# Two of eight Strassen pairs in plain products, in an attention and feed-forward kernel on one core

## The chip, the cores and the metric

The kernel runs on one core of one Trainium2 chip. The metric is the device time of one execution in microseconds (us); 727.54 us is the median of three runs of the kernel before (723.6 to 728.09).

## The reference

Eight batches of 8 heads, 576 tokens, head dimension 64, with 32 packed queries `p` per head. Two attentions in a row, then a feed-forward net with ELU on all 4608 tokens:

```
p_packed = softmax(p k^T / 8) v             # per batch and head: 32 x 64
x = softmax(q p_packed^T / 8) p_packed      # per batch and head: 576 x 64
h = x @ w_in                                # 4608 x 512 @ 512 x 2048
g = where(h > 0, h, exp(min(h, 0)) - 1)
out = g @ w_out                             # 4608 x 2048 @ 2048 x 512
```

The weights arrive as 64-bit floats, all else as 32-bit ones.

## The kernel before

**Products.** A product of 32-bit numbers is made of three fast ones: each operand is split into a high part that the fast format holds and the low rest, and high x high, high x low and low x high are added in PSUM. The kernel multiplies the packed values with `w_in` first (`mstep`, L788), so `h` is the product of this matrix `m` (as `m_hi`, `m_lo`) with the second attention's weights `a` (`a_hi`, `a_lo`).

**Tiling.** 2048 hidden columns are 16 f tiles of 128 (`NF`), and a batch's 576 tokens are two windows. A stretch is one window through all f tiles. For even batches the windows have 256 and 320 tokens, for odd ones 320 and 256; the 64 tokens over 256 of an even batch are kept after ELU (`half_sb`) and finished with the 320 of the next odd batch's first window. Batches 0 and 1 are interleaved (`VISITS`), while weights are still being converted; from batch 2 on a stretch is 16 steps in a row.

**Plain steps.** One f tile: `h` into a PSUM bank (L1185, 6 matmuls), ELU on ACT and DVE, the split of `g`, and per 128 tokens three matmuls of 512 columns (`out_mm`, L1309 to L1312), summed over f in one bank per 128 tokens.

**Strassen pairs.** Seven stretches, those with 256 tokens to finish from batch 2, window 1, to batch 6, window 1, take two f tiles at a time (`strassen_pair`, L957): 256 tokens x 256 hidden by 256 hidden x 512 columns is a 2 x 2 product of blocks, made with seven block products instead of eight (Winograd's form). `g`'s sums are made on DVE (`sums`, L1049), high and low parts of seven blocks on ACT and DVE (`hi`, L277, and `lo`, L1055), and 21 matmuls of 256 columns (L1096) add into four banks (`acc`). They are issued in four groups, each an operation of its own. After the eighth pair DVE puts the banks together (L1122) in `part`, and one store (L1149) writes 256 rows.

**Sums of `w_out`.** Of the seven right-hand blocks three are in `w_out` itself (`own`) and four are sums. `strassen_weights` (L889) makes the sums once a pair, 32 tiles of 256 KB in all, and stores them in DRAM (`sw_dram`, L932); each stretch loads them again (L1068) into a ring of six buffers (`sw`).

**Order.** Nothing is scheduled by hand. Each operation gets a priority (`prio`, about the step at which it is due), a cost on the engines that it may run on, what it waits for and the buffers that it takes, and `schedule()` (L165) plays the program through with these costs: a free engine takes the first operation in order of priority that is ready. `LAG` is the time after an operation's end until others may use its result, 2.2 us for a DMA. The order found is written out, and on the chip each engine runs its own list in order, waiting by semaphores. SP issues nearly all DMAs, so a DMA that waits on SP holds those behind it. Due times are numbers: `T_ATT` and `T_ATTS` for the six parts of a batch's attention (`ts`: keys, transposes, value products, the transpose of the packed values, two halves of the scores), `TM` and `TMS` for `mstep`, `T_SW` for the weights' sums, `T_SL` for how many steps ahead the sums are loaded, `LOOK_S` for how late the output products are due, `T_SE` for the last additions.

**Keys, values, queries.** From batch 1 on they are loaded in halves of 576 KB into a ring of two buffers (`kvq`): keys (L458), values (L465), queries (L477). So value loads wait for the first scores (L505, L546), query loads for the value products (L642), and the next keys for the second scores (L687).

Of the kernel before, what the change touches and what calls it, by code (L numbers as in the profile page):

```python
# [20 lines left out]
def packed_attention_elu_ffn(  # L21
# [22 lines left out]
    nc = tc.nc  # L44
# [36 lines left out]
    T_ATT, T_ATT1 = [12, 14.0, 15.0, 16.0, 17.5, 17.5], [-12, -11, -11, -10, -10, -9]  # L81
    LI, LO, LM, LOOK = 4.5, 3.0, 2.5, 3.5
    TM = [24.5, 24.5, 28.0, 28.5]
# [10 lines left out]
    T_ATTS = [[10, 8, 12.5, 11.5, 12.0, 16.5], [-4, -2, 1, 8, 18, 24.0]]  # L94
    TMS = [[22, 22, 28, 28], [25, 29, 31.5, 32.0]]
    S_FIRST, T_SW, T_SL, T_SE, LOOK_S = (2, 1), 20, 2, 4, 3.5
# [58 lines left out]
    def op(prio, on, fn, deps=(), take=(), use=(), after=(), mode=None):  # L155
        o = Op()
        o.prio, o.on, o.fn, o.deps = prio, on, fn, [d for d in deps if d is not None]
        o.after = [d for d in after if d is not None]
        o.take, o.end, o.n, o.mode = list(take), None, len(ops), mode
        for b in list(take) + list(use):  # L160
            b.users.append(o)
        ops.append(o)
        return o

    def schedule():  # L165
# [19 lines left out]
        while todo:  # L185
            for n, o in enumerate(todo[:400]):
# [14 lines left out]
                o.start, o.end = now, now + cost + LAG[e]  # L201
# [194 lines left out]
    def attention(b, ts):  # L396
# [542 lines left out]
    for u in range(NF // 2):  # L939
        strassen_weights(u)  # L940
# [16 lines left out]
    def strassen_pair(i, b, win, f):  # L957
# [92 lines left out]

        def hi(e):
            copy(e, g_b.all[:, :7 * P], blocks(1, 8))

        def lo(e):
            nc.vector.tensor_tensor(  # L1055
                out=g_b.all[:, 7 * P:], in0=blocks(1, 8), in1=g_b.all[:, :7 * P].bitcast(F32),
                op=ALU.subtract,
            )

        last = f + 2 == NF  # L1060
        x = op(i + 1, {"DVE": 0.95}, sums, done, use=[w8])
        x = run["g"] = op(i + 1, {"ACT": 0.95}, hi, [x], take=[g_b], use=[w8], after=[run["g"]])
        x = op(i + 1, {"DVE": 1.09}, lo, [x], use=[g_b, w8])
        sw = [sw_buf() for _ in range(4)]
        ld = {}
        for n in (2, 1, 0, 3):
            def load(e, n=n):
                nc.sync.dma_start(out=sw[n].t.bitcast(F32), in_=sw_dram[u, n])  # L1068

            ld[n] = run["sw"] = op(  # L1070
                i - T_SL, {"DMA": 0.7}, load, [s_ready[u, n]], take=[sw[n]], after=[run["sw"]]
            )
# [4 lines left out]
        def own(f, n):  # L1077
            return None, lambda part: wo(f, part)[:, n * H:(n + 1) * H]

        if f == 0:  # L1080
            run["acc"] = [banks(1) for _ in range(4)]
        acc = run["acc"]

        groups = (
            ((1, own(f, 0)),),
            ((6, t(2)), (3, own(f + 1, 0))),
            ((5, t(1)), (4, t(0))),
            ((2, t(3)), (7, own(f + 1, 1))),
        )
        for a, group in zip(acc, groups):  # L1090

            def mm(e, a=a, group=group):
                for n, (blk, (_, y)) in enumerate(group):
                    for k, (p, q) in enumerate(((0, 0), (0, 1), (1, 0))):
                        x0 = (7 * p + blk - 1) * P
                        nc.tensor.matmul(  # L1096
                            a.t[:, n * H:(n + 1) * H], lhsT=g_b.all[:, x0:x0 + P], rhs=y(q),
                            start=f == 0 and n == k == 0,
                            stop=last and k == 2 and n == len(group) - 1,
                        )  # L1100

            ns = [y[0] for _, y in group if y[0] is not None]
            run["out"] = op(
                i + 1 + LOOK_S, {"PE": 0.355 * len(group)}, mm, [x] + [ld[n] for n in ns],
                take=[a] if f == 0 else [],
                use=[g_b] + [sw[n] for n in ns] + ([] if f == 0 else [a]), after=[run["out"]],
            )
            a.last = run["out"]
        if last:
# [5 lines left out]
            def two(x):  # L1115
                return x.unsqueeze(1).to_broadcast([P, 2, H])

            def bank(n):
                return acc[n].t.rearrange("p (n e) -> p n e", e=H)

# [4 lines left out]
            def first(e):  # L1125
                copy(e, part.t[:, :H], acc[0].t[:, :H])

            def add1(e):
                add(slots(1, 1)[:, :2], two(part.t[:, :H]), bank(1))

            def add2(e):
                add(slots(0, 3), two(part.t[:, H:2 * H]), bank(2))

            def add3(e):
                add(part.t[:, H:2 * H], part.t[:, :H], acc[2].t[:, H:])

            def add4(e):
                add(slots(0, 3), slots(0, 3), bank(3))
# [3 lines left out]
            y = op(q, {"ACT": 0.35, "DVE": 0.4}, first, [acc[0].last], take=[part], use=acc[:1])  # L1142
            y = op(q, {"DVE": 0.69}, add1, [y, acc[1].last], use=[part, acc[1]])
            y = op(q, {"DVE": 0.69}, add2, [y, acc[2].last], use=[part, acc[2]])
            y = op(q, {"DVE": 0.42}, add3, [y], use=[part, acc[2]])
            y = op(q, {"DVE": 0.69}, add4, [y, acc[3].last], use=[part, acc[3]])

# [263 lines left out]
```

## Time and profile before

| what | us |
|---|---|
| median of three runs | 727.54 |
| the profiled execution's own time | 725.27 |
| its span, first to last instruction | 723.1 |
| PE busy in it (matmuls) | 694.2 |
| DVE busy | 572.7 |
| ACT busy | 437.6 |

The span is cut by what runs: loads and the first softmax to about 25 us, batches 0 and 1 with the weights' conversion, plain and Strassen stretches in turn after them, Strassen ones between 265 and 641 us, and the last window of batch 7 in plain steps to the end. PE is TensorE's matmuls, PEld its weight loads, DVE VectorE, ACT ScalarE, SP the engine that issues DMAs (SPq is its queue). A row of a group gives line, engine, operation, tiles written and read, shape and count, then busy us and the mean ns of one, then idle us ahead of them and what ended it.

### The profile page before, as it was taken

The numbers are of one execution on the slowest core, as the hardware profiler recorded it, in microseconds if no ns is written. First come the engines' busy times: TensorE is split into PE (matmuls) and PEld (weight loads), VectorE is DVE, ScalarE is ACT, GpSimd is POOL, SyncE is SP. The second block draws the span as 40 slices with busy tenths as digits, with TensorE's granted clock in tenths as the row PEclk, the third lists the DMA queues.
The fourth block names the chain that finished last, engine by engine and source line by source line (L and its number), as shares of the span: only waits on it lengthen the run. The fifth ranks groups of instructions, "written<-read, shape, count | busy, mean of one in ns | idle before, by whom it ended". The sixth has DMA issues, their size and how long they took to land.

```text
span 723.1 us, 14717 instructions
## 1 busy us (share of the span) xinstructions
PE 694.2 (96%) x5580; PEld 572.6 (79%) x5580; DVE 572.7 (79%) x1318; ACT 437.6 (61%) x936; POOL 19.4 (3%) x27
## 2 busy tenths in 40 slices
PE   2799999999998999999999999999999999999997
PEld 1445588887776888988888898888888898988886
DVE  6999998888999899755887788965787789874453
ACT  5777888786766576635566446645367556654332
POOL 0000002110111000000000000000000000000000
PEclk9999999999999999999999999999999999999999
DMA  9846546535759576705377998532468887620010
GB/s 349 292 155 206 182 145 146 132 65 126 211 108 306 213 241 206 240 4 156 112 233 233 323 289 274 183 130 67 135 197 263 284 285 256 211 82 1 0 44 30
DMA packets 66262, 128.62 MB, mean 178 GB/s; under 512 B 6544, under 2 KB 16016, under 8 KB 65936
## 3 DMA queue, kind: packets, MB, share of 16 engines
q1 hardware_dynamic: 63168, 122.18, 51.2%
q0 software_dynamic: 3024, 5.51, 5.3%
q8 instruction: 44, 0.72, 0.4%
q14 instruction: 26, 0.21, 0.1%
HBM read 104.33 MB, written 23.33 MB: 177 GB/s over the span
## 4 chain that ended last, share of the span: by engine, by line
PE 90%; DMA 6%; DVE 2%; ACT 1%; issue 0%; SPq 0%; ACTq 0%
PE psum L1096 19%; PE psum L1185 14%; PE psum L979 11%; PE psum L1309 10%; PE psum L1310 10%; PE psum L1312 10%; PE psum L1295 4%; PE psum L788 4%; DMA sw<-sw_dram 3%; DMA kvq<-in_qT 2%; PE psum L1178 2%; PE psum L642 2%; PE psum L616 1%; PE psum L687 1%; DMA k<-in_kT 1%; PE psum L546 1%
## 5 line engine op out<-in xcount | busy, mean ns | idle before, releaser
L1192 ACT ACTIVATE e<-psum 128x320 f32<-128x320 f32 (+1 forms) x144 | 59.9, 416 | 75.0 <-PE psum L1185 64.0
L1096 PE MATMUL psum<-sw,g 128*128 128x256 f32 x672 | 101.5, 284 | 3.6 <-DMA sw<-sw_dram 3.6
L1096 PEld LDWEIGHTS psum<-sw,g 128*128 128x128 f32 x672 | 88.4, 189 | 9.8 <-issue 6.0
L1201 DVE SCALAR_TENSOR_TENSOR e<-e,psum 128x256 f32<-128x256 f32 (+1 forms) x128 | 57.3, 447 | 30.0 <-ACT e L1198 29.4
L1185 PE MATMUL psum<-a_hi,m_hi 128*128 128x320 f32 (+1 forms) x256 | 79.7, 311 | 0.0
L1185 PE MATMUL psum<-a_lo,m_hi 128*128 128x320 f32 (+1 forms) x256 | 76.4, 298 | 0.0
L1185 PE MATMUL psum<-a_hi,m_lo 128*128 128x320 f32 (+1 forms) x256 | 76.3, 298 | 0.0
L1309 PE MATMUL psum<-wo_b,g 128*128 128x512 f32 x174 | 70.1, 403 | 0.0
L1310 PE MATMUL psum<-wo_b,g 128*128 128x512 f32 x174 | 68.7, 395 | 0.0
L979 PE MATMUL psum<-a_hi,m_hi 128*128 128x256 f32 (+1 forms) x224 | 67.1, 299 | 0.2 <-DVE half_sb L986 0.2
L1055 DVE TENSOR_TENSOR g<-w,g 128x896 fp32r<-128x896 f32 x56 | 60.3, 1083 | 8.4 <-ACT g L277 8.2
L1224 DVE TENSOR_TENSOR g<-e,g 128x256 fp32r<-128x256 f32 (+1 forms) x128 | 58.0, 453 | 10.7 <-ACT g L277 8.9
L277 ACT CAST g<-w 128x896 fp32r<-128x896 f32 x56 | 52.6, 939 | 22.7 <-DVE w L1049 15.9
L1198 ACT ACTIVATE e<-e 128x320 f32<-128x320 f32 (+1 forms) x144 | 64.7, 449 | 2.6
L979 PE MATMUL psum<-a_lo,m_hi 128*128 128x256 f32 (+1 forms) x224 | 65.8, 294 | 0.0
L979 PE MATMUL psum<-a_hi,m_lo 128*128 128x256 f32 (+1 forms) x224 | 65.7, 293 | 0.0
L1049 DVE TENSOR_TENSOR w<-w 128x128 f32<-128x128 f32 x168 | 56.0, 333 | 4.5
L1185 PEld LDWEIGHTS psum<-a_hi,m_hi 128*128 128x128 f32 x256 | 48.5, 189 | 10.8 <-issue 1.1
L1310 PE MATMUL psum<-wo_a,g 128*128 128x512 f32 x140 | 55.5, 396 | 0.0
L1309 PE MATMUL psum<-wo_a,g 128*128 128x512 f32 x140 | 55.4, 396 | 0.0
L1185 PEld LDWEIGHTS psum<-a_lo,m_hi 128*128 128x128 f32 x256 | 48.6, 190 | 4.5 <-issue 1.0
L1312 PE MATMUL psum<-wo_b,g 128*128 128x512 f32 x174 | 52.1, 395 | 0.0
(130 smaller groups left out, 1486.0 us busy)
## 6 DMA issues: line engine op xcount, KB each, us to landing
sw<-sw_dram SPq DMA_DIRECT2D x224, 256.0 KB, 3.7
raw<-in_w_in SPq DMA_DIRECT2D x16, 512.0 KB, 4.1
kvq<-in_v SPq DMA_DIRECT2D x16, 512.0 KB, 5.3
raw<-in_w_out SPq DMA_DIRECT2D x16, 512.0 KB, 3.5
sw_dram<-sw SPq DMA_DIRECT2D x32, 256.0 KB, 4.1
kvq<-in_kT SPq DMA_DIRECT2D x14, 576.0 KB, 4.9
kvq<-in_qT SPq DMA_DIRECT2D x14, 576.0 KB, 5.4
out<-part SPq DMA_DIRECT2D x21, 256.0 KB, 2.3
```

Source lines behind the costliest of these rows:

```text
L979: nc.tensor.matmul(ps, lhsT=m_b[p].t[:, g, o:o + P], rhs=st.a.t[q][:, g, cols], start=(n == 0), stop=(n == 3 * G - 1),)
L1049: nc.vector.tensor_tensor(out=out, in0=x, in1=y, op=o)
L1055: nc.vector.tensor_tensor(out=g_b.all[:, 7 * P:], in0=blocks(1, 8), in1=g_b.all[:, :7 * P].bitcast(F32), op=ALU.subtract,)
L1096: nc.tensor.matmul(a.t[:, n * H:(n + 1) * H], lhsT=g_b.all[:, x0:x0 + P], rhs=y(q), start=f == 0 and n == k == 0, stop=last and k == 2 and ...
L1185: nc.tensor.matmul(ps_b.t[:, :n_tok], lhsT=m_b[x].t[:, g, o:o + P], rhs=st.a.t[y][:, g, cols], start=(n == 0), stop=(n == 3 * G - 1),)
L1192: nc.scalar.activation(out=e_b.t[:, :n_tok], in_=ps_b.t[:, :n_tok], func=AF.Relu, scale=-1.0)
L1198: nc.scalar.activation(out=x, in_=x, func=AF.Exp, scale=-1.0)
L1201: nc.vector.scalar_tensor_tensor(out=out, in0=e_b.t[:, cs], scalar=-1.0, in1=ps_b.t[:, cs], op0=ALU.add, op1=ALU.max)
L1224: nc.vector.tensor_tensor(out=g_b.t[1][:, cs], in0=x, in1=g_b.t[0][:, cs].bitcast(F32), op=ALU.subtract)
L1309: nc.tensor.matmul(a.t, lhsT=g_b.t[0][:, t], rhs=wo(f, 0), start=first, stop=False)
L1310: nc.tensor.matmul(a.t, lhsT=g_b.t[0][:, t], rhs=wo(f, 1), start=False, stop=False)
L1312: nc.tensor.matmul(a.t, lhsT=g_b.t[1][:, t], rhs=wo(f, 0), start=False, stop=final)
```

## The change

In each Strassen stretch pairs 0 and 7 (`S_PLAIN`) go without the scheme. Their four blocks of `g` are split as they are (512 columns instead of 896), and twelve matmuls of 512 columns, in two groups, add the first 128 tokens' products into bank 3 and the others' into bank 2. The sums of `w_out` for these two pairs are neither made, stored nor loaded. In the other pairs the seven products are shared out among the four banks in another way, so that banks 2 and 3 hold whole halves of the result; the last additions are six instead of five. A bank is taken by the first pair that uses it.

Loads of sums are called eight steps ahead (`T_SL` 2 to 8), output products are due six steps late instead of 3.5 (`LOOK_S`), and the planner counts a load of sums with 0.8 us on the DMA and 1.5 us more until it can be used (`lag`); the same 1.5 us and a higher cost stand for keys, values and queries from batch 3 on. The due times of attention, of `mstep`, of the weights' sums and of the last additions have new numbers.

```diff
-    T_ATT, T_ATT1 = [12, 14.0, 15.0, 16.0, 17.5, 17.5], [-12, -11, -11, -10, -10, -9]
+    T_ATT, T_ATT1 = [12, 14.0, 14.5, 15.5, 17.0, 17.0], [-12, -11, -11, -10, -10, -9]
...
-    T_ATTS = [[10, 8, 12.5, 11.5, 12.0, 16.5], [-4, -2, 1, 8, 18, 24.0]]
-    S_FIRST, T_SW, T_SL, T_SE, LOOK_S = (2, 1), 20, 2, 4, 3.5
+    S_PLAIN = [0, 7]
+    T_ATTS = [[9, 7, 11.5, 8.5, 13.0, 21.5], [-4, -2, -2, 3, 14.5, 20.5]]
+    S_FIRST, T_SW, T_SL, T_SE, LOOK_S = (2, 1), 17, 8, 3, 6.0
...
-                o.start, o.end = now, now + cost + LAG[e]
+                o.start, o.end = now, now + cost + LAG[e] + o.lag
...
-                    t, {"DMA": 3.3 / len(bufs)}, lambda e, fn=fn, n=n: fn(e, n),
+                    t, {"DMA": (3.3 if b < 3 else 3.8) / len(bufs)}, lambda e, fn=fn, n=n: fn(e, n),
                     take=[x] + ([p_b] if (name, n) == ("k", 0) else []), after=[prev_ld],
+                    lag=1.5 * (b > 2),
...
     for u in range(NF // 2):
-        strassen_weights(u)
+        if u not in S_PLAIN:
+            strassen_weights(u)
...
+        plain = u in S_PLAIN
+        b0, b1 = (0, 4) if plain else (1, 8)
         def hi(e):
-            copy(e, g_b.all[:, :7 * P], blocks(1, 8))
+            copy(e, g_b.all[:, :(b1 - b0) * P], blocks(b0, b1))
...
-        x = op(i + 1, {"DVE": 0.95}, sums, done, use=[w8])
+        if not plain:
+            done = [op(i + 1, {"DVE": 0.95}, sums, done, use=[w8])]
...
+        if not plain:
+            sw = [sw_buf() for _ in range(4)]
+            for n in (2, 1, 0, 3):
...
+                ld[n] = run["sw"] = op(
+                    i - T_SL, {"DMA": 0.8}, load, [s_ready[u, n]], take=[sw[n]], after=[run["sw"]],
+                    lag=1.5,
+                )
...
         groups = (
-            ((1, own(f, 0)),),
-            ((6, t(2)), (3, own(f + 1, 0))),
-            ((5, t(1)), (4, t(0))),
-            ((2, t(3)), (7, own(f + 1, 1))),
+            ((1, own(f, 0), 0), (6, t(2), 1)),
+            ((5, t(1), 0), (4, t(0), 1)),
+            ((3, own(f + 1, 0), 0), (7, own(f + 1, 1), 1)),
+            ((2, t(3), 0),),
         )
+        if plain:
+            groups = (
+                (), (), ((1, own(f, 0, 2), 0), (3, own(f + 1, 0, 2), 0)),
+                ((0, own(f, 0, 2), 0), (2, own(f + 1, 0, 2), 0)),
+            )
...
+            cost = 1.386 if plain else 0.355 * len(group)
...
             def add4(e):
-                add(slots(0, 3), slots(0, 3), bank(3))
+                add(part.t[:, 2 * H:], part.t[:, 2 * H:], acc[2].t)
+
+            def add5(e):
+                n = 2 * H if S_PLAIN else H
+                add(part.t[:, :n], part.t[:, :n], acc[3].t[:, :n])
```

More of the change, by code (lines that the diff above doesn't have):

```diff
@@ L1061, in strassen_pair @@
-        x = op(i + 1, {"DVE": 0.95}, sums, done, use=[w8])
-        x = run["g"] = op(i + 1, {"ACT": 0.95}, hi, [x], take=[g_b], use=[w8], after=[run["g"]])
-        x = op(i + 1, {"DVE": 1.09}, lo, [x], use=[g_b, w8])
-        sw = [sw_buf() for _ in range(4)]
-        ld = {}
[L1066 to L1072, printed above, removed]
+                out=g_b.all[:, 7 * P:(7 + b1 - b0) * P], in0=blocks(b0, b1),
@@ L1113, in slots @@
                 return part.t.rearrange("p (n e) -> p n e", e=H)[:, n::step]
[L1115 to L1119, printed above, removed]
             def add(out, x, y):
```

68 lines of the change are left out of this document (42 added, 26 removed).

## The prediction

> **What bounds the kernel now.** I read the page first, then the stretches in time, then PE's waits, then the timeline at the two places where PE stood still.
>
> ```profile
> span 723.1 us, 14717 instructions
> PE 694.2 (96%) x5580; PEld 572.6 (79%) x5580; DVE 572.7 (79%) x1318; ACT 437.6 (61%) x936; POOL 19.4 (3%) x27
> core 0: us, PE busy (x) PEld busy (x) DVE busy (x) ACT busy (x) POOL busy (x), PEclk, DMA share, GB/s
> 0.00:25.00 25.00, 10.00 (x187) 5.93 (x187) 18.70 (x44) 15.99 (x31) 0.69 (x6) 1.00 0.93 346
> 25.00:227.00 202.00, 198.84 (x1509) 143.16 (x1510) 183.29 (x430) 152.72 (x360) 18.12 (x21) 0.99 0.59 161
> 227.00:235.00 8.00, 5.14 (x44) 4.08 (x42) 7.66 (x20) 4.81 (x16) 0.63 (x1) 0.97 1.06 336
> 235.00:265.00 30.00, 30.00 (x199) 24.89 (x183) 25.66 (x64) 19.07 (x49) 0.00 (x0) 0.95 0.61 216
> 265.00:641.00 376.00, 371.98 (x3256) 327.07 (x3249) 296.65 (x657) 215.14 (x407) 0.00 (x0) 1.00 0.63 203
> 641.00:723.10 82.10, 78.22 (x414) 67.43 (x412) 40.71 (x109) 29.91 (x76) 0.00 (x0) 1.00 0.06 23
> PE psum L1096 <- DMA sw<-sw_dram: 3.6, 6, 0.9
> PE psum L687 <- DMA kvq<-in_qT: 3.0, 2, 2.9
> ```
>
> PE is busy in 694.2 of 723.1 us. Of the 28.9 us without work, 15.0 lie in the first 25 us (loads and the first softmax), 3.9 after 641 us and 3.2 from 25 to 227 us; PE's order is the same in both kernels up to about 215 us. Left for this change are two places: 227 to 235 us, where 2.9 us are lost, and the Strassen stretches, 265 to 641 us, where 376.00 - 371.98 = 4.0 us are lost. The last two rows (total, times, longest) say to what: 2.9 us once to a load of queries, 3.6 us in six waits for Strassen sums read back from DRAM. DVE and ACT are not named, so work taken from them is worth nothing by itself.
>
> At the first place the wait costs more than its own length (timeline: start, time; then windows, with the granted clock third from the end):
>
> ```profile
> 231.34 0.27 PE L668 MATMUL psum<-ident,pp 128*128 128x128 f32 x1
> 234.47 1.18 PE L687 MATMUL psum<-kvq,ppT 64*32 64x288 f32 x16 [2.86 <-DMA kvq<-in_qT]
> 235.95 0.41 PE L1185 MATMUL psum<-a_lo,m_hi 128*128 128x256 f32 x1
> ...
> 240.35 0.28 PE L1185 MATMUL psum<-a_lo,m_hi 128*128 128x256 f32 x1
> 235.00:237.00 2.00, 2.00 (x22) 1.43 (x7) 0.66 (x2) 0.00 (x0) 0.00 (x0) 0.50 1.07 393
> 237.00:239.00 2.00, 2.00 (x9) 1.63 (x8) 0.58 (x3) 1.71 (x6) 0.00 (x0) 0.75 0.90 293
> ```
>
> After 2.86 us without work the granted clock is 0.50 from 235 to 237 us and 0.75 from 237 to 239, and the same matmul that takes 0.28 us at 240 takes 0.41. That is 2 x 0.50 + 2 x 0.25 = 1.5 us more.
>
> **The plain pairs.** The change turns 2 of 8 pairs in each of 7 stretches, 14 pairs, from 21 matmuls of 256 columns into 12 of 512. Their spacing, from starts in quiet places:
>
> ```profile
> 299.72 0.52 PE L1096 MATMUL psum<-wo_b,g 128*128 128x256 f32 x3
> ...
> 301.84 0.52 PE L1096 MATMUL psum<-wo_b,g 128*128 128x256 f32 x3
> 302.19 0.31 PE L1185 MATMUL psum<-a_hi,m_hi 128*128 128x320 f32 x1
> ...
> 647.48 0.39 PE L1309 MATMUL psum<-wo_a,g 128*128 128x512 f32 x1
> ...
> 648.86 0.84 PE L1312 MATMUL psum<-wo_a,g 128*128 128x512 f32 x3
> 649.54 0.30 PE L1185 MATMUL psum<-a_hi,m_hi 128*128 128x320 f32 x1
> L1310 PEld LDWEIGHTS psum<-wo_b,g 128*128 128x128 f32 x174 | 32.8, 189 | 5.0
> ```
>
> A Strassen pair's 21 matmuls (3, 15 left out, 3) take 302.19 - 299.72 = 2.47 us, 0.118 each. Nine of 512 columns (one each at 647.48, 647.71, and so on, then three) take 649.54 - 647.48 = 2.06 us, 0.229 each. A plain pair then takes 12 x 0.229 = 2.75 us, 0.28 more, and all of it is on PE, which is the path: 14 x 0.28 = **+3.9 us**. Rounding of starts makes this 3.5 to 4.3. The weight load of 189 ns lies under both; with plain pairs it lies wholly under its 229 ns.
>
> The Trainium skill (TensorE: Matmul & The Clock Gate, Back-to-back issue gap) gives another spacing for a stream of loads and matmuls, about 131 ns at 512 columns and 81 at 128. By it a plain pair would take 12 x 0.131 = 1.6 us and the change would gain on PE. This trace shows 229 ns, and the sum goes by the trace.
>
> **What leaves DVE, ACT and the queue.** Per plain pair the three sums go, and the split shrinks from 896 to 512 columns:
>
> ```profile
> L1049 DVE TENSOR_TENSOR w<-w 128x128 f32<-128x128 f32 x168 | 56.0, 333 | 4.5
> L1055 DVE TENSOR_TENSOR g<-w,g 128x896 fp32r<-128x896 f32 x56 | 60.3, 1083 | 8.4 <-ACT g L277 8.2
> L277 ACT CAST g<-w 128x896 fp32r<-128x896 f32 x56 | 52.6, 939 | 22.7 <-DVE w L1049 15.9
> L1122 DVE TENSOR_TENSOR part<-part,psum 128x512 f32<-128x512 f32 x21 | 14.4, 685 | 3.5 <-PE psum L1096 2.8 <-ACT e L1192 0.5
> sw<-sw_dram SPq DMA_DIRECT2D x224, 256.0 KB, 3.7
> ```
>
> DVE saves 56.0 / 56 = 1.0 us of sums and 1.08 - 0.69 = 0.4 us of split a pair, 14 x 1.4 = 20 us; the result of a stretch costs it one more addition of 256 columns, less than 0.69 us, 7 times. ACT saves about 14 x 0.94 x 384/896 = 5.6 us. Neither is waited for, so I cost all of it at nothing; if DVE were late somewhere it would only help. Of the read-backs 56 of 224 go, and 8 of 32 stores, for two pairs need no sums in DRAM.
>
> **The query load.** Keys, values and queries take turns in two buffers (kvq), so queries can load only after the products with the values (L642). SP's queue at this place, before, from the value loads of batch 3 to its query load and behind:
>
> ```order
> L465 DMA kvq<-in_v 128x2x512
> L469 DMA kvq<-in_v 64x256
> L932 DMA sw_dram<-sw 128x512 x8
> L477 DMA kvq<-in_qT 128x4x288 x2
> L932 DMA sw_dram<-sw 128x512 x4
> L454 DMA p<-in_pT 128x128
> ```
>
> and now (the same lines, 3 or 4 further down; L1083 is the load of sums, formerly L1068):
>
> ```order
> L468 DMA kvq<-in_v 128x2x512
> L472 DMA kvq<-in_v 64x256
> L936 DMA sw_dram<-sw 128x512 x5
> L480 DMA kvq<-in_qT 128x4x288 x2
> L936 DMA sw_dram<-sw 128x512 x8
> L1083 DMA sw<-sw_dram 128x512 x2
> ```
>
> The query load has moved ahead of three of the stores. PE's order has moved more. What stands at the first scores of batch 3 (L687), before:
>
> ```order
> L1185 MATMUL psum<-a_lo,m_hi 128x256
> L1185 MATMUL psum<-a_hi,m_lo 128x256
> L668 MATMUL psum<-ident,pp 128x128
> L687 MATMUL psum<-kvq,ppT 32x288 x8
> L1185 MATMUL psum<-a_hi,m_hi 128x256
> ```
>
> and now (L691 is the former L687, L1215 the former L1185, L1339 the former L1309):
>
> ```order
> L1215 MATMUL psum<-a_lo,m_hi 128x256
> L1215 MATMUL psum<-a_hi,m_lo 128x256
> L691 MATMUL psum<-kvq,ppT 32x288 x8
> L1339 MATMUL psum<-wo_b,g 128x512
> L1340 MATMUL psum<-wo_b,g 128x512
> ```
>
> The scores no longer follow the transpose (L668) at once. Between value products and scores stood 18 matmuls of 256 and 18 of 512 columns, 18 x 0.118 + 18 x 0.229 = 6.2 us; now stand 60 and 54, 19.4 us. The chain of waits has the load, from issue to landing, as:
>
> ```profile
> 226.85 7.49 DMA kvq<-in_qT
> ```
>
> 7.5 us fit under 19.4 and did not fit under 6.2. So the 2.9 us go, and with them the 1.5 us of half clock: **-4.4 us**. Later batches' query waits were 3.0 - 2.9 = 0.1 us, nothing. What is late next there is the softmax of batch 3 on DVE, begun some 20 us later; its result is read only by the stretch of batch 3, behind the whole Strassen stretch of batch 2.
>
> **The read-backs.** They use six buffers, four a pair, and SP issues one when the load six places earlier has been read. Eight steps instead of two cannot change that; what changes is how far PE's order holds the use from that reading. Counted along PE's order at the spacings above (0.147 for 320 columns), the shortest distance from freeing to use was 3.6 us, five of the loads had under 4.0; now the shortest is 4.2. The median landing is 3.7 us. The worst waits were of another kind, behind queries and a result:
>
> ```profile
> 395.86 1.73 SPq L477 DMA_DIRECT2D kvq<-in_qT  x2
> 397.69 0.56 SPq L1068 DMA_DIRECT2D sw<-sw_dram  x1
> 399.66 0.39 SPq L1149 DMA_DIRECT2D out<-part  x1
> 400.15 3.23 SPq L1068 DMA_DIRECT2D sw<-sw_dram  x5
> 404.55 0.59 PE L1096 MATMUL psum<-sw,g 128*128 128x256 f32 x3 [0.92 <-DMA sw<-sw_dram]
> SPq L1068 <- PE psum L1096: 27.0, 30, 4.1
> ```
>
> The queue at that place (stretch of batch 4, window 0, into window 1), before:
>
> ```order
> L1068 DMA sw<-sw_dram 128x512 x14
> L477 DMA kvq<-in_qT 128x4x288 x2
> L1068 DMA sw<-sw_dram 128x512
> L1149 DMA out<-part 128x2x512
> L1068 DMA sw<-sw_dram 128x512 x7
> ```
>
> and now (L480 for L477, L1179 for the result's store L1149):
>
> ```order
> L1083 DMA sw<-sw_dram 128x512 x6
> L480 DMA kvq<-in_qT 128x4x288 x2
> L1083 DMA sw<-sw_dram 128x512 x3
> L1179 DMA out<-part 128x2x512
> L1083 DMA sw<-sw_dram 128x512 x11
> ```
>
> The queries now stand where plain pairs 7 and 0 run, 12 matmuls each that read nothing back: the six loads around them have 12 to 17 us from freeing to use; before, the loads there had 5 to 9. I take two thirds of the 3.6 us as gone, **-2.4 us**; the bounds are nothing and all of it, and 1.2 us stay at the loads with 4.2 to 5 us behind the key loads.
>
> **Sum.** +3.9 - 4.4 - 2.4 = -2.9 us. The profiled execution took 725.27 us (span 723.1 and 2.2 around it), so its like would take 722.4. The runs shown were 723.6, 727.54 and 728.09, so the profiled one lies 2.3 under the median; an after in the same spread has a median of 722.4 to 724.6. I say **723**.
>
> **Rivals.** (1) The loads are called earlier but can't go earlier, and the read-back waits stay, for six buffers are what holds them: the row of 27.0 us shows SP itself waiting for PE to free buffers, 30 times in 55 us. Then the sum is +3.9 - 4.4 = -0.5: 724.8 to 727. For it speaks that the loads still go out at the freeing; against it the longer distances. The Trainium skill (Perfetto Trace Analysis, Optimization Strategy) reads a gap that repeats on the busy engine as a sign of too few buffers; by that rule calling loads earlier gains nothing, and this rival is its case here. Chance 0.2.
>
> (2) Slower: the result store between the two Strassen windows holds the queue. It waits for DVE's additions, now six in a row instead of five, the last two after the plain pair's groups, and eleven read-backs stand behind it. Before, the additions were through soon after the last group:
>
> ```profile
> 396.94 0.51 PE L1096 MATMUL psum<-wo_b,g 128*128 128x256 f32 x3
> 398.40 1.20 DVE L1122 TENSOR_TENSOR part<-part,psum 128x256 f32<-128x256 f32 x2
> ```
>
> The store went out at 399.66, 2.2 us after that group ended at 397.45. From the last plain group to the first use of a load behind the store stand 66 matmuls of 256, 7.8 us. A load needs 3.7, so it decides from 4.1 us of delay on. If DVE held the store for 8 us, PE would lose some 4 us at each of two such places and 1.5 of half clock each, 11 us: 722.4 + 11 = 733. Against it: DVE has 1.4 us less a pair there. Chance 0.1.
>
> (3) The wide matmuls run at the rate of their weight loads, 189 ns: 12 x 0.189 - 2.47 = -0.2 us a pair, 14 times -2.8 instead of +3.9, 715.7. The 229 ns rows speak against it. This is the place of the skill's rule on spacing. Chance 0.03.
>
> (4) All waits go and the runs fall near the lower edge: +3.9 - 4.4 - 3.6 = -4.1, 721.2, less what spread gives. Chance 0.12; the forecast has 0.55.
>
> **Numbers.** The range, 718 to 729, takes in the forecast, (1), (4) and the spread of 723.6 to 728.09 around them; (2) and (3) are left out. A measurement here tells about 1%, 7.3 us, from no change. Faster by more: (3), and an after whose runs happen to lie low against a high before, 0.15. Slower by more: (2), 0.1. The rest, 0.75, is within.
>
> **What would show it.** PE's matmuls 5580 - 126; no idle before the scores of batch 3 and no granted clock of 0.50 after 30 us but at the end; plain pairs at 2.75 us; waits for read-backs near 1.2 us; the store between windows out within 4 us of the last plain group. The forecast is wrong if PE's idle time from 265 to 641 us grows over 4.0 us, or if a new wait of over 2.8 us halves the clock elsewhere.

## The result, and the profile after

The changed kernel takes 717.97 us (median of four runs, 717.22 to 719.71), the kernel before beside it 727.55 (723.6 to 728.09). The ratio is 0.988 with a 95% interval of 0.985 to 0.992: faster by 1.2%, where 723 was forecast and "faster by over 1%" had a chance of 0.15. The median lies 0.03 us under the lower edge of the range of 718 to 729, and the gain of 9.6 us between the medians is about twice the 4.5 us forecast.

The profiled execution took 718.22 us. The page's span and engines:

```profile
span 716.1 us, 14260 instructions
PE 692.8 (97%) x5454; PEld 567.2 (79%) x5454; DVE 554.8 (77%) x1279; ACT 425.0 (59%) x916; POOL 19.5 (3%) x27
```

The windows (length, busy of PE, PEld, DVE, ACT and POOL, then granted clock, DMA share, GB/s):

```profile
25.00:227.00 202.00, 198.05 (x1490) 142.96 (x1494) 182.02 (x427) 151.09 (x357) 17.90 (x20) 0.99 0.58 160
227.00:235.00 8.00, 8.00 (x80) 6.97 (x69) 7.22 (x19) 6.41 (x21) 0.86 (x1) 1.00 0.94 215
235.00:265.00 30.00, 30.00 (x191) 25.47 (x190) 25.71 (x64) 17.75 (x44) 0.00 (x0) 1.00 0.60 210
265.00:641.00 376.00, 375.83 (x3151) 324.88 (x3150) 285.64 (x633) 207.48 (x401) 0.00 (x0) 1.00 0.51 163
641.00:716.10 75.10, 70.72 (x375) 60.87 (x373) 35.58 (x95) 26.30 (x67) 0.00 (x0) 1.00 0.05 18
```

And what is left of PE's waits for queries and read-backs (total, times, longest):

```profile
PE psum L691 <- DMA kvq<-in_qT: 0.3, 1, 0.3
PE psum L1120 <- DMA sw<-sw_dram: 0.2, 1, 0.2
```

PE's waits are gone at both places that the prediction named: from 227 to 235 us PE is busy all 8.00 us (5.14 before), and from 265 to 641 us it lacks 0.17 us (4.02 before). From 25 to 227 us PE lacks 0.8 us more than before, after 641 us 0.5 more, in the first 25 us 0.1 less, so idle time went from 28.9 to 716.1 - 692.8 = 23.3 us, 5.6 less.

**The span lost more than idle time.** It lost 7.0 us. By the forecast's terms busy time should have risen by the plain pairs' 3.9 and fallen by the 1.5 of half clock, to 696.6; it is 692.8. So 3.8 us more went out of what the page calls busy. The timeline of before shows how that can be; these are the two matmuls ahead of the longest read-back wait, which the prediction's row at 404.55 ends:

```profile
403.24 0.28 PE L979 MATMUL psum<-a_lo,m_hi 128*128 128x256 f32 x1
403.36 0.28 PE L979 MATMUL psum<-a_hi,m_lo 128*128 128x256 f32 x1
```

In a quiet place one matmul of 256 columns starts 0.12 us after the other, yet each is shown as 0.28 us long. From 403.36 to 404.55 are 1.19 us, so 1.19 - 0.12 = 1.07 us were lost; the row says 0.92, for it counts from the shown end. So at 256 columns a wait is shown about 0.16 us too short, and one under 0.16 doesn't show at all. So I added up start-to-start times over all matmuls, less the quiet spacing of their shape (0.119 us for 256 columns, 0.147 for 320, 0.231 for 512):

| us lost | before | after | difference |
|---|---|---|---|
| 220 to 240 us (query wait, half clock) | 6.0 | 1.2 | -4.8 |
| 240 to 640 us | 29.6 | 22.6 | -7.0 |
| of these, gaps behind a read-back | 4.6 | 0.3 | -4.3 |
| the rest | 28.8 | 29.4 | +0.6 |
| all | 64.4 | 53.2 | -11.2 |

The small matmuls of the attention stand in both columns alike, so only the differences are read. With 3.8 us more of columns the last one is -7.4, and the spans differ by 7.0.

### The profile page after: what moved, and what is told of

It is laid out like the page before. It is cut to its first block, busy times and chain, and to the rows that moved or that the text cites. A ratio compares the mean times of both kernels' runs of the same rounds, so it can differ in the third digit from the quotient of the medians.

```text
span 716.1 us, 14260 instructions
## 1 busy us (share of the span) xinstructions
PE 692.8 (97%) x5454; PEld 567.2 (79%) x5454; DVE 554.8 (77%) x1279; ACT 425.0 (59%) x916; POOL 19.5 (3%) x27
## 4 chain that ended last, share of the span: by engine, by line
PE 94%; DMA 3%; DVE 1%; ACT 1%; issue 0%; SPq 0%; ACTq 0%
PE psum L1120 20%; PE psum L1215 15%; PE psum L984 12%; PE psum L1339 10%; PE psum L1340 10%; PE psum L1342 10%; PE psum L1325 4%; PE psum L792 4%; PE psum L1208 2%; PE psum L646 2%; PE psum L620 1%; DMA k<-in_kT 1%; PE psum L691 1%; DMA kvq<-in_qT 1%; PE psum L550 1%; DMA sw<-sw_dram 1%
## 5 line engine op out<-in xcount | busy, mean ns | idle before, releaser
L1120 PE MATMUL psum<-sw,g 128*128 128x256 f32 x504 | 78.9, 284 | 0.2 <-DMA sw<-sw_dram 0.2
L1120 PEld LDWEIGHTS psum<-sw,g 128*128 128x128 f32 x504 | 67.4, 189 | 7.9 <-issue 4.7
L1063 DVE TENSOR_TENSOR g<-w,g 128x896 fp32r<-128x896 f32 (+1 forms) x56 | 55.1, 984 | 15.3 <-ACT g L280 14.3
L280 ACT CAST g<-w 128x896 fp32r<-128x896 f32 (+1 forms) x56 | 48.1, 858 | 27.6 <-DVE w L1054 11.9
L1120 PE MATMUL psum<-wo_b,g 128*128 128x256 f32 (+1 forms) x273 | 50.7, 318 | 0.0
```

What stands on the lines that cost most here:

```text
L280: (nc.scalar.copy if e == "ACT" else nc.vector.tensor_copy)(out=out, in_=in_)
L1063: nc.vector.tensor_tensor(out=g_b.all[:, 7 * P:(7 + b1 - b0) * P], in0=blocks(b0, b1), in1=g_b.all[:, :(b1 - b0) * P].bitcast(F32), op=ALU ...
L1120: nc.tensor.matmul(a.t[:, at * H:at * H + rhs.shape[-1]], lhsT=operand(blk, p), rhs=rhs, start=a.first == u and n == k == 0, stop=a.final ...
```

## The experiments

In the expectations A is the prediction's account: due times and order take PE's waits away, and a plain pair only costs PE its 0.28 us. B and D are stated in the expectations themselves; C was formed after e1 to e4. The kernels stood beside the kernel before in three groups (e1 to e4, e5 to e8, e9 to e12), so across groups the ratios are compared.

| kernel | median us | ratio, 95% interval | span of the profile |
|---|---|---|---|
| e1 no plain pair | 724.60 | 0.998, 0.995 to 1.000 | 725.1 |
| e2 plain pairs, old numbers | 726.28 | 1.000, 0.998 to 1.003 | 723.2 |
| e3 before, query load told right | 722.54 | 0.995, 0.992 to 0.998 | 724.6 |
| e4 loads two steps ahead | 720.92 | 0.992, 0.988 to 0.995 | 715.6 |
| e5 the changed kernel again | 719.71 | 0.989, 0.987 to 0.992 | 718.0 |
| e6 pair 0 alone plain | 716.98 | 0.986, 0.984 to 0.989 | 715.4 |
| e7 idle sums of `g` | 720.46 | 0.991, 0.988 to 0.993 | 718.3 |
| e8 idle sums of `w_out` | 722.59 | 0.993, 0.990 to 0.996 | 721.4 |
| e9 pair 0 plain in one stretch | 723.89 | 0.997, 0.995 to 0.999 | 721.8 |
| e10 no allowance for read-backs | 718.60 | 0.991, 0.988 to 0.994 | 716.5 |
| e11 no plain pair, sums early | 729.11 | 1.003, 1.001 to 1.005 | 726.4 |
| e12 products due earlier | 720.41 | 0.993, 0.990 to 0.996 | 720.8 |

### The query wait by itself (e3)

The kernel before, in which the planner takes the query load of batch 3 for 4 us longer (`op` and `schedule()` get `lag` as in the change, left out here):

```diff
...
                     take=[x] + ([p_b] if (name, n) == ("k", 0) else []), after=[prev_ld],
+                    lag=4.0 * (b == 3 and name == "q"),
```

> The kernel before, in which the planner counts 4 us more until the query load of batch 3 can be used and nothing else is changed: its first scores then stand 10 us behind the value products instead of 5, the order from the first Strassen stretch on keeps its distances. Theory A: the 2.86 us wait at 231 us and the 1.5 us of half clock behind it go, 4.4 us: 727.5 - 4.4 = 723, and read-back waits stay at 3.6 us. Rival: PE finds the next wait right there (softmax of batch 3 later, another load), and the time is within 1 us of before, 727. If the wait goes but the clock dips elsewhere, 724.6.

Measured 722.54 us, 0.995: 3.6 us faster (1.7 to 5.5). Its window at the place, and then its waits for read-backs and queries:

```profile
227.00:235.00 8.00, 8.00 (x94) 6.90 (x83) 7.25 (x18) 5.92 (x18) 0.86 (x1) 1.00 1.08 304
```

```profile
PE psum L1098 <- DMA sw<-sw_dram: 3.9, 6, 1.3
PE psum L689 <- DMA kvq<-in_qT: 1.8, 2, 1.3
```

The 2.86 us and the half clock are gone, the six read-back waits stand, and a later query wait of 1.3 us is new. The profiled execution is the slowest of its twelve (726.85 us), and in it PE lacks 0.84 us from 235 to 265 us, mostly waiting for DVE, and 5.61 us from 265 to 641 (4.02 before). So the 3.6 us are what is left after new losses. The term of 4.4 us lies within their interval, and nothing but one load's planned length is needed to take that wait away.

### Which half of the change (e1, e2)

The new numbers without plain pairs, and the plain pairs with all the old numbers (`T_ATT`, `TM` and the costs of loads too, left out here):

```diff
-    S_PLAIN = [0, 7]
+    S_PLAIN = []
```

```diff
-    T_ATTS = [[9, 7, 11.5, 8.5, 13.0, 21.5], [-4, -2, -2, 3, 14.5, 20.5]]
-    TMS = [[22, 19.5, 26.5, 26.5], [24, 28, 31.0, 31.5]]
-    S_FIRST, T_SW, T_SL, T_SE, LOOK_S = (2, 1), 17, 8, 3, 6.0
+    T_ATTS = [[10, 8, 12.5, 11.5, 12.0, 16.5], [-4, -2, 1, 8, 18, 24.0]]
+    TMS = [[22, 22, 28, 28], [25, 29, 31.5, 32.0]]
+    S_FIRST, T_SW, T_SL, T_SE, LOOK_S = (2, 1), 20, 2, 4, 3.5
...
-                    lag=1.5,
+                    lag=0,
```

> The changed kernel with S_PLAIN empty: all eight pairs keep Strassen's scheme, the new due times, calls and allowances stay. Theory A (the forecast's terms: plain pairs cost PE 3.9 us, the waits went because the new due times and the longer allowance for a load moved uses away from loads): 3.9 us less on PE; value products to scores of batch 3 are 15 us apart in PE's order, so the query wait and the half clock stay away; the loads of sums have 34 of 224 uses under 5 us from freeing to use (12 of 168 in the changed kernel, 62 of 224 before), so 1 to 2 us of read-back waits come back: about 718 - 3.9 + 1.5 = 715 to 716, faster than the changed kernel. Theory B (the waits went because two pairs of eight read nothing back: less traffic, room at the ends of a stretch): read-back waits return to 3.6 us or more and eat the 3.9: 718 to 720.

> The change with the old numbers: plain pairs 0 and 7 and the new sharing of banks, but due times, two steps ahead, LOOK_S 3.5 and the DMA costs without extra allowance as before. Theory A: PE +3.9 us; scores of batch 3 now stand 13.6 us behind the value products, so the 4.4 us of query wait and half clock go all the same; shortest distance from freeing to use 3.7 us, 12 of 168 under 4.5, so some 2 us of read-back waits stay: 727.5 + 3.9 - 4.8 - 2 = 724 to 725. Theory B: the plain pairs do it all, 718 to 720.

Neither half is worth much: 724.60 us (0.998) and 726.28 us (1.000), where the whole change gives 0.988. For e1 both expected times were 4 us or more too low, and with them the step that plain pairs only cost PE: without them PE has 3.9 us less to do, and the kernel is some 6 us slower. Its query wait stays away. In its place stands a new one; the timeline of PE, and then the two windows around it:

```profile
265.71 0.50 PE L1120 MATMUL psum<-wo_a,g 128*128 128x256 f32 x2 [1.25 <-ACT g L280]
266.93 0.58 PE L1120 MATMUL psum<-wo_a,g 128*128 128x256 f32 x1 [0.71 <-DVE g L1063]
```

```profile
235.00:265.00 30.00, 28.86 (x183) 23.71 (x181) 28.58 (x74) 18.43 (x49) 0.00 (x0) 1.00 0.78 277
265.00:275.00 10.00, 8.57 (x43) 8.37 (x44) 8.53 (x22) 4.38 (x9) 0.00 (x0) 0.66 0.52 170
```

At the first Strassen pair of the program PE waits for `g`, and the granted clock is 0.66 over ten us behind it, 3.4 us lost. DVE, which PE's waits of before name with 0.2 us twice, is busy 28.58 of the 30 us ahead (25.71 after the change): there the sums of `w_out`, the softmax of batch 3 and the first `g` of the scheme come together. In e2, with the old numbers, PE waits elsewhere for DVE and for read-backs, and lacks 4.97 us in the Strassen stretches. Its query wait is gone too; theory A had 724 to 725 for it, and the 2.9 us of waits for DVE, which A put at nothing, are enough to make the difference:

```profile
PE psum L984 <- DVE half_sb L991: 2.9, 4, 0.8
PE psum L1120 <- DMA sw<-sw_dram: 1.6, 2, 1.2
```

```profile
265.00:641.00 376.00, 371.03 (x3108) 320.41 (x3107) 276.00 (x611) 206.82 (x401) 0.00 (x0) 1.00 0.51 162
```

So I formed theory C: the plain pairs pay by what they take off DVE, and the new due times can only be kept with that.

### Where DVE's relief counts (e5 to e8)

First the mark, the changed kernel once more:

> The changed kernel itself once more, as the mark for the three beside it and to see how far two profiles of the same kernel differ. Both theories: 717 to 720 us, 1.0 to 1.5% under the kernel before.

719.71 us, 0.989. Its span is 1.9 us longer than that of the first profile, though PE's idle time behind 227 us agrees within 0.1 us; the windows at the start, of the first profile and of this one, show where from:

```profile
25.00:40.00 15.00, 11.53 (x144) 7.89 (x145) 14.00 (x33) 10.53 (x27) 0.00 (x0) 0.89 0.75 265
```

```profile
25.00:40.00 15.00, 12.22 (x137) 7.57 (x138) 11.95 (x28) 8.72 (x22) 0.00 (x0) 0.66 0.65 225
```

A mean granted clock of 0.89 is 0.11 short of full and half clock 0.5 short, so the clock was at half for 15 x 0.11 x 2 = 3.3 us in the one and for 15 x 0.34 x 2 = 10.2 us in the other. Spans of single profiles are compared below only where these windows agree, or by stretch.

e7 lets DVE make the three sums of `g` in the plain pairs too, where nothing reads them:

```diff
         def lo(e):
+            if plain:
+                sums(e)
```

> The changed kernel, but in the plain pairs DVE also makes the three sums of g that nothing reads there (1.0 us, 14 times, between the high and the low part); PE's order is the same. Theory A (work on DVE is worth nothing): PE's waits do not grow by more than 1 us, time within 1 us of the changed kernel. Theory C (DVE's relief in the stretches is what pays): DVE is late at the pairs behind, PE waits for g or w on DVE grow by 3 us or more, 721 us or more. Theory C narrowed to the place near 265 us, where the sums of w_out meet the softmax: same as A here.

720.46 us, 0.75 over e5 and within the spread of both (718.93 to 721.09 against 718.03 to 721.16). In the Strassen stretches DVE has the work, and PE does not feel it:

```profile
265.00:641.00 376.00, 375.92 (x3146) 324.30 (x3145) 296.38 (x670) 208.23 (x401) 0.00 (x0) 1.00 0.51 163
```

DVE is busy 296.38 us for 285.64, and PE is short by 0.08 us. So for the sums of `g` the prediction's "cost all of it at nothing" holds, and C in its wide form, which has these sums pay too, is wrong.

e8 makes and stores the sums of `w_out` for all eight pairs, two of them for nothing:

```diff
-        if u not in S_PLAIN:
-            strassen_weights(u)
+        strassen_weights(u)
```

> The changed kernel, but the sums of w_out are made and stored for all eight pairs, those of pairs 0 and 7 for nothing (DVE some 2 x 5 us more, eight stores of 256 KB more before 265 us). Theory A: within 1 us of the changed kernel. Theory C narrowed to this place: DVE is full from 235 to 265 us, PE waits over 1 us for g or w near 264 us, and the granted clock is halved behind it, together +3 to +6 us: 721 to 724.

722.59 us, 2.9 over e5. PE's longest wait behind 227 us, and then the windows:

```profile
270.08 0.38 PE L1119 MATMUL psum<-wo_a,g 128*128 128x256 f32 x1 [0.98 <-DVE g L1062]
```

```profile
235.00:265.00 30.00, 29.27 (x182) 23.87 (x182) 28.71 (x73) 19.07 (x50) 0.00 (x0) 1.00 0.79 274
265.00:275.00 10.00, 8.81 (x62) 7.66 (x68) 9.79 (x25) 5.99 (x13) 0.00 (x0) 1.00 0.42 146
```

DVE is busy 28.71 of 30 us, and PE is short by 0.73 + 1.19 = 1.92 us where it was short by nothing: the wait of e1 is back at its place, though all plain pairs stay. The clock was not halved this time. e8 also stores the eight tiles, and its DMA share at the place is 0.79 (0.60 after the change); e9 below has the wait with a share of 0.60, so the stores are not needed for it. So C holds at this place.

e6 leaves only pair 0 plain:

```diff
-    S_PLAIN = [0, 7]
+    S_PLAIN = [0]
```

> Only pair 0 goes without the scheme; pair 7 is back in it. Seven plain pairs less at 0.28 us each: -1.9 us on PE. Theory A (the gain is order and early loads, plain pairs only cost PE): about 2 us faster than the changed kernel, 716. Theory C (plain pairs pay by relief of DVE): half the relief is gone, seven more pairs with 1.0 us of sums and 0.4 us more split on DVE, and one more pair's sums of w_out at 235 to 265 us; waits of PE for DVE or ACT come back in part and eat the 1.9 us: 718 to 721, equal to the changed kernel or slower.

716.98 us (716.23 to 718.78), 2.7 under e5 and the fastest of all, 0.986 of the kernel before (0.984 to 0.989). Part of this is the start: e6's five executions all have a mean granted clock of 0.998, e5's six 0.991 to 0.998. The changed kernel's six executions at 0.997 and more, of both groups, took 718.1 us in the mean, e6's five 717.2, so about 0.9 of the 2.7 us are left for pair 7. Against the first profile of the changed kernel, whose start has the same clock, the span is 0.7 us shorter, 715.4 for 716.1. Seven pairs at 0.28 us are 1.9 us, and some of it goes to waits near 265 us:

```profile
235.00:265.00 30.00, 30.00 (x190) 25.32 (x189) 27.43 (x69) 19.44 (x51) 0.00 (x0) 1.00 0.71 244
265.00:275.00 10.00, 9.45 (x83) 8.62 (x81) 9.09 (x22) 6.57 (x15) 0.00 (x0) 1.00 0.50 161
```

Half the relief (DVE 27.43) leaves 0.55 us of wait; of the other 0.6 us, 0.17 are a wait at 230 us, and the rest I can't place. A's time of about 716 came out; of C the wait near 265 us came back in part, but too small to eat the gain. Pair 7 in plain products is a price with little for it; pair 0 pays, since without it (e1) the ratio is 0.998.

### Two ways to keep the scheme (e9, e11)

If only the sums before 265 us mattered, pair 0 need be plain in the first stretch alone:

```diff
-    S_PLAIN = [0, 7]
+    S_PLAIN = {S: [0] for S in [(2, 1)]}
...
-        prio = s_first + f - T_SW
+        prio = s_first + (f or 2 * NF) - T_SW
...
-    for u in range(NF // 2):
-        if u not in S_PLAIN:
-            strassen_weights(u)
+    turns = [*range(1, NF // 2), 0]
+    for u in turns:
+        strassen_weights(u)
...
-        plain = u in S_PLAIN
+        plain = u in S_PLAIN.get((b, win), [])
...
```

> Pair 0 goes without the scheme in the first Strassen stretch alone; the sums of w_out for pair 0 are made later, for the second stretch. Theory C narrowed (what pays is that DVE has fewer sums to make before 265 us): the waits near 265 us stay away, and six plain pairs less than with pair 0 everywhere are worth 6 x 0.28 = 1.7 us: about 715, the fastest so far. Rival D (pair 0 pays in every stretch, by the loads and queries it gives room to): waits for read-backs or queries come back in the later stretches, 717 to 720.

723.89 us, 0.997: 9 us over the expectation of C, beyond D too. The edit did not do what I meant. A priority doesn't hold an operation back; a planner that gives a free engine the first ready operation put the late sums where DVE seemed free. Of the sums' low parts (one for each 256 columns) DVE makes 20 between 225 and 268 us in e9, as many as in e1 and e8; e6 has 16 and the changed kernel 12. The group of e9, the wait of PE, and the windows:

```profile
L931 DVE TENSOR_TENSOR sw<-w,sw 128x256 fp32r<-128x256 f32 x20 | 7.8, 418 | 0.8 <-ACT sw L280 0.8
```

```profile
265.78 0.38 PE L984 MATMUL psum<-a_hi,m_hi 128*128 128x320 f32 x1 [1.91 <-DVE w L991]
```

```profile
235.00:265.00 30.00, 28.87 (x181) 23.78 (x180) 28.87 (x71) 18.54 (x51) 0.00 (x0) 1.00 0.60 204
265.00:275.00 10.00, 8.83 (x62) 7.69 (x63) 9.69 (x25) 5.44 (x11) 0.00 (x0) 0.83 0.83 280
```

So five kernels with the new numbers stand in a row at this place: 12 and 16 sums, PE short by 0 and 0.55 us; 20 sums, short by 1.92, 2.30 and 2.57, with half clock behind two of the three. That pair 0 itself was plain in e9 did not help there.

The number of sums is not the whole of it: e3 and e11 have 20 in the same time too, and PE waits less in them. What the profiles of all kernels but e11 line up by is how busy DVE is at the place, whichever numbers and pairs they have:

| DVE busy, 235 to 265 us | kernels | PE without work, 235 to 275 us |
|---|---|---|
| 25.7 to 26.8 | before, after, e4, e5, e7, e10, e12 | 0 |
| 27.4 to 27.9 | e2 (0.3 us of it a read-back), e3, e6 | 0.6 to 0.8 |
| 28.6 to 28.9 | e1, e8, e9 | 1.9 to 2.6 |

In e11 the long query wait falls into this time, and DVE idles with PE. The kernel before, with all eight pairs' sums, stands in the first row: there the sums came earlier.

But e9 also loses later, and that speaks for D. From 275 to 641 us, e6, then e9 and its waits for read-backs:

```profile
275.00:641.00 366.00, 365.89 (x3141) 319.01 (x3140) 284.49 (x633) 206.01 (x392) 0.00 (x0) 1.00 0.57 183
```

```profile
275.00:641.00 366.00, 363.24 (x3190) 319.18 (x3190) 286.13 (x634) 208.32 (x397) 0.00 (x0) 1.00 0.63 202
```

```profile
PE psum L1120 <- DMA sw<-sw_dram: 1.6, 3, 0.8
```

2.76 us are missing where e6 misses 0.11: 1.6 in read-back waits and 1.1 in two waits for DVE, at 421 us (0.6) and 604 us (0.4). e1 and e11, which have no plain pair, show the same two waits for DVE. So the plain pair in the later stretches seems to pay as well: the loads at their seams, where one Strassen stretch passes into the next, have 12 matmuls of 512 columns to hide under, and DVE has less to do there. e9's order differs from e6's in other places too, so this is argued, not shown. Against e6, e9 gains 6 x 0.28 = 1.7 us of columns and loses 2.30 - 0.55 = 1.75 near 265 us, 10 x 0.17 = 1.7 to half clock and 2.65 later. That is 4.4 net of the 6.4 us between the spans; where the other 2 lie is not shown.

e11 keeps the scheme everywhere and moves the sums forward, out of the softmax's way:

```diff
-    S_PLAIN = [0, 7]
+    S_PLAIN = []
-    S_FIRST, T_SW, T_SL, T_SE, LOOK_S = (2, 1), 17, 8, 3, 6.0
+    S_FIRST, T_SW, T_SL, T_SE, LOOK_S = (2, 1), 20, 8, 3, 6.0
```

> No plain pair, and the sums of w_out due 20 steps ahead as in the kernel before, where the changed numbers have 17. The sums then stand ahead of the softmax of batch 3 on DVE, and ahead of its query load on SP; between the value products and the scores of batch 3 stand 5.2 us of other matmuls. Theory C as a conflict of two jobs on DVE between 225 and 265 us: the waits near 265 us go, the query wait near 231 us (2 to 3 us, and 1.5 us or more of half clock) returns; 719 to 723, and no value of this number would give both. Theory A (only the place of the sums was wrong): neither wait, 715 to 716.

729.11 us, 1.003 (1.001 to 1.005), the slowest. As C had it, the query wait is back, and longer, with more half clock; the scores in the timeline, then two windows:

```profile
236.76 1.22 PE L691 MATMUL psum<-kvq,ppT 64*32 64x288 f32 x16 [3.61 <-DMA kvq<-in_qT]
```

```profile
235.00:239.00 4.00, 2.24 (x21) 1.35 (x22) 1.99 (x5) 0.00 (x0) 0.00 (x0) 0.56 1.03 380
239.00:243.00 4.00, 4.00 (x13) 3.24 (x13) 2.25 (x8) 2.01 (x6) 0.00 (x0) 0.59 0.66 207
```

3.61 us of wait and 4 x 0.44 + 4 x 0.41 = 3.4 of clock. The waits near 265 us shrank but did not go (0.96 us are missing from 265 to 275), and from 275 to 641 us 2.53 us are missing, so the time fell 6 us above the 719 to 723 expected. With eight pairs' sums and the other new numbers, one value of `T_SW` gives the wait at 265 us and the other the query wait. With the old numbers it is otherwise: e3 makes all eight pairs' sums, has no wait there, and lacks 0.84 us from 235 to 265 us. That no value between or beyond would do better is not shown; 17 and 20 are what was run.

### What took the read-back waits away (e4, e10, e12)

Three numbers of the changed kernel, each set back alone: `T_SL` to 2, the planner's allowance for a read-back to none, `LOOK_S` to 3.5:

```diff
-    S_FIRST, T_SW, T_SL, T_SE, LOOK_S = (2, 1), 17, 8, 3, 6.0
+    S_FIRST, T_SW, T_SL, T_SE, LOOK_S = (2, 1), 17, 2, 3, 6.0
```

```diff
-                    i - T_SL, {"DMA": 0.8}, load, [s_ready[u, n]], take=[sw[n]], after=[run["sw"]],
-                    lag=1.5,
+                    i - T_SL, {"DMA": 0.7}, load, [s_ready[u, n]], take=[sw[n]], after=[run["sw"]],
+                    lag=0,
```

```diff
-    S_FIRST, T_SW, T_SL, T_SE, LOOK_S = (2, 1), 17, 8, 3, 6.0
+    S_FIRST, T_SW, T_SL, T_SE, LOOK_S = (2, 1), 17, 8, 3, 3.5
```

> The changed kernel with its sums called two steps ahead (T_SL 8 to 2), all else as changed. Theory A, with six buffers as the limit: the loads go out when a buffer comes free, whenever they are called; distances from freeing to use are the same (shortest 4.25 us, 10 of 168 under 5), so the time is that of the changed kernel within 1 us, 718. Rival: the earlier call is what hid the read-backs; then they wait again, 3 us or more: 721 and up.

> The changed kernel, but the planner counts a read-back as before (0.7 us on the DMA, no 1.5 us more). Along PE's order eight loads then have under 4.5 us from freeing to use, the shortest 3.7; with the allowance the shortest is 4.25. If the allowance is what keeps the read-backs away from their use: read-back waits of 1 to 2 us return, 719 to 722. If the other numbers do it: within 1 us of the changed kernel.

> The changed kernel, but output products due 3.5 steps late as before instead of six. Along PE's order the shortest distance from freeing to use is 4.6 us, so read-back waits should not return. If LOOK_S does nothing else: 717.5 to 720, the same as the changed kernel. If later products were what gave DVE time for g: waits of PE for g on DVE of 1 us or more, 720 to 723.

720.92, 718.60 and 720.41 us; the intervals of the ratios 0.992, 0.991 and 0.993 overlap with that of e5's 0.989. e4 and e12 lie 2.9 and 0.4 us above the times expected if nothing else changed; their waits do not say why. In their PE waits a read-back stands only in e10, with 0.2 us:

```profile
PE psum L1120 <- DMA sw<-sw_dram: 0.2, 1, 0.2
```

None of the three is what did it. Calling the loads eight steps ahead, which the description of the change names, moves no wait that can be measured: the ring of six buffers sets when a load goes. The waits are gone in e1 as well (0.2 us, no plain pair), smaller in e2 (1.6, old numbers), e9 (1.6) and e11 (1.3). That leaves the rest of the new order, the due times of attention and of `mstep` included; which of those numbers carries it stays open.

## Why the prediction was right, and where it was wrong

**Plain pairs, +3.9 us: right.** Two of them at the seam between batch 4's windows, with what starts behind each:

```profile
391.68 2.96 PE L1120 MATMUL psum<-wo_b,g 128*128 128x512 f32 x12
394.47 0.28 PE L984 MATMUL psum<-a_hi,m_hi 128*128 128x256 f32 x1
...
395.89 2.91 PE L1120 MATMUL psum<-wo_a,g 128*128 128x512 f32 x12
398.64 0.28 PE L984 MATMUL psum<-a_hi,m_hi 128*128 128x256 f32 x1
```

2.79 and 2.75 us from start to start, 2.75 forecast, and 5454 matmuls are 5580 - 126. That is 229 ns and more a matmul: rival (3) falls, and with it, for this kernel's high and low parts of 32-bit numbers, the 131 ns of the Trainium skill (TensorE: Matmul & The Clock Gate, Back-to-back issue gap).

**Query load, -4.4 us: right in size, with a slip in its working.** The trace gives -4.8, e3 -3.6 by itself. Between value products and scores stood 12 matmuls of 512 columns before, not the 18 that the prediction counted, so its 6.2 us were 18 x 0.118 + 12 x 0.229 = 4.9; the load's 7.49 us fit under neither, and nothing else hung on it. The half clock cost 1.7 us, not 1.5: the windows began at 235 us, and it had begun before:

```profile
234.00:239.00 5.00, 4.53 (x29) 3.29 (x30) 2.24 (x7) 1.71 (x6) 0.00 (x0) 0.66 1.00 355
```

5 x 0.34 = 1.7. After the change no granted clock under 1.00 is left there:

```profile
235.00:237.00 2.00, 2.00 (x13) 1.76 (x12) 1.11 (x4) 0.69 (x3) 0.00 (x0) 1.00 1.08 410
```

**Read-backs, -2.4 us: right in kind, too small.** I took two thirds of 3.6 us. All but 0.2 went, and the 3.6 were 4.6 by start-to-start times: -4.3. That no early call is needed was right (e4). The reason given, a longer shortest distance along PE's order, is not shown: e2 and e10 both have 3.7 us by their expectations, close to the 3.6 of before, and PE waits 1.6 us in one and 0.2 in the other. Rival (1), which had the waits stay because the six buffers do, falls: the ring is as it was, and the waits are gone. The Trainium skill's reading of a repeated gap as too few buffers (Perfetto Trace Analysis, Optimization Strategy), which says "can mean", did not apply: here another order of the work cured it.

**Short gaps, not costed.** Some 2.7 us more went between 240 and 640 us in gaps that the page counts as busy. The prediction worked from idle rows and could not see them; what made them shorter is not shown. With the 1.9 us more at the read-backs, less the 0.6 us by which the other stretches are worse, this is about what the forecast of 722.4 for a like profile lacked to 718.22.

**"Neither is waited for, so I cost all of it at nothing": the step that failed.** The rows of before did name no DVE, but they showed an order with other due times. In the new order the sums of `w_out` stand beside the softmax of batch 3, and with them all PE waits there: 12 sums no wait, 20 sums 1.9 to 2.6 us, and half clock behind two of three (e1, e8, e9). Of what leaves DVE the prediction listed the sums and the split of `g`, but not the sums of `w_out` themselves, only their stores and loads. This was the part that counted; in the profile of before:

```profile
L927 DVE TENSOR_TENSOR sw<-w,sw 128x256 fp32r<-128x256 f32 x32 | 12.3, 417 | 0.0
L903 DVE TENSOR_TENSOR w<-w 128x512 f32<-128x512 f32 x8 | 5.5, 683 | 0.0
L897 DVE TENSOR_TENSOR w<-wo_a 128x1024 f32<-128x1024 f32 x4 | 4.9, 1219 | 0.0
L897 DVE TENSOR_TENSOR w<-wo_b 128x1024 f32<-128x1024 f32 x4 | 4.9, 1216 | 0.0
L913 DVE TENSOR_TENSOR w<-w,w 128x256 f32<-128x256 f32 x8 | 3.4, 425 | 0.3
L910 DVE TENSOR_TENSOR w<-w,w 128x256 f32<-128x256 f32 x8 | 3.4, 419 | 0.0
```

That is 34.4 us for eight pairs, 4.3 a pair. The prediction even named that softmax as late next, and called it harmless because its result is read late; it is not its result that is late but `g` behind it on DVE. The forecast's sum came through because the change brought both, so that the waits it left out did not arise. The part of the step that concerns `g`'s own sums holds (e7).

**Rival (2), the store that holds the queue: wrong.** SP at the seam of batch 4, after the change:

```profile
389.79 1.82 SPq L480 DMA_DIRECT2D kvq<-in_qT  x2
391.71 1.52 SPq L1083 DMA_DIRECT2D sw<-sw_dram  x3
395.39 0.39 SPq L1179 DMA_DIRECT2D out<-part  x1
400.99 10.44 SPq L1083 DMA_DIRECT2D sw<-sw_dram  x11
```

The last plain group ends at 394.47 and the store goes at 395.39, 0.9 us behind it. The next loads go at 400.99, when PE frees buffers, not when the store lets them; SP's waits from 396 to 402 us:

```profile
SPq L1083 <- PE psum L1120: 5.8, 2, 5.5
```

**The median.** I set 0.6 us on top of 722.4 because the profiled run of before lay under its median. The measured medians differ by 9.6 us and the two profiled spans by 7.0; e5's span alone is 1.9 off its twin. One profile is no better than about 2 us here. That the median came out at the edge of the range is partly the terms' doing, too small at the read-backs and blind to short gaps, and partly chance: the same kernel's median was 719.71 in e5.

## What to carry to other kernels

An engine that nobody waits for has slack under the order that was profiled and under no other: when a change takes work from it and also moves the order, cost both together, by the densest 30 us of that engine and not by its mean share. Waits read from shown ends are too short, by 0.16 us each here at 256 columns; with many short gaps start-to-start times give the better sum. And a number that asks for something earlier is worth nothing where a ring of buffers decides when it can be had.

## What the runs showed of the hardware that I had not expected

The clock's price of a wait comes in steps here. Half clock cost 1.7 us behind a wait of 2.86 us (before), 10 x 0.17 = 1.7 behind 1.91 us (e9), 3.4 behind 1.25 and 0.71 us in a row (e1) and 3.4 behind 3.61 us (e11). It cost nothing behind 0.98 us (e8), nor behind the two single waits of 1.3 us in e3, whose granted clock is 1.00 from 265 to 641 us. The prediction took 2.8 us as the length from which a wait does so; 1.9 was enough. The Trainium skill (TensorE: Matmul & The Clock Gate, Part 1) has the clock fall after at least one idle window of about 3.4 us; the waits of 1.9 and 2.86 us disagree with that as a least length, while losses near 1.7 and 3.4 us, half of one and of two such windows, fit its length.

The same kernel's start ran at half clock for 3.3 us in one profile and 10.2 in another (the two windows of e5), and the spans differ by 1.9 us. In e1, e4 and e11 the granted clock is 1.00 from 25 to 40 us. The same section of the Trainium skill says that the windows run free and that the cold stretch at a start varies from run to run; these profiles agree in that it varies.
